# The seven-product last stage of a fused attention and two-MLP kernel: GpSimd's work moved to VectorE, other memory, other banks

## The chip, the cores and the metric

The kernel runs on one core of a Trainium2 chip. The metric is the device time of one execution in microseconds, the median of 3 runs. One more execution was taken by the profiler; its trace is what is read below. TensorE is called PE, VectorE DVE, ScalarE ACT, GpSimd POOL, SyncE SP.

## The reference, cut to what matters

Three blocks follow each other: attention with a memory term, an MLP, and a second MLP without an activation but with a product of two projections.

```python
x = attention(q, k, v, M_prev, z_prev, beta)          # (2304, 512)
h = x @ w_in                                          # 512 -> 2048
x2 = (h * np.tanh(np.log1p(np.exp(np.minimum(h, 20.0))))) @ w_out   # 2048 -> 512
a = x2 @ w1                                           # 512 -> 1024
b = x2 @ w2                                           # 512 -> 1024
out = ((a * b) @ w3) @ w_out2                         # 1024 -> 1024 -> 512
```

Inputs come as doubles and are decoded to float32 on the chip. Each float32 operand of a matmul is split into a rounded high part and a low part (high plus low is the value), and a product of two operands is made of three matmuls: high with high, high with low, low with high.

## The kernel before

The first MLP runs in four quarters of its 2048 columns (`emit_h`, `emit_x2`, the gate). Beside the last quarter a generator, `fold`, makes `w3 @ w_out2` (1024 x 512) in 32 pieces: decode (`decode`, L87 to L107: six DVE instructions and one POOL add per piece, three buffers for the loads), transpose, split, eight accumulated steps, then `wo` (L600 to L606), which has one buffer, is copied by ACT and DVE and stored to `w_dram`. When all is stored, `wft` is loaded from `w_dram` in two halves of two 1 MB loads (L657), into the memory that held `w_out2`, so the first half starts when the fold's last matmul is done.

The last stage then works on `x2` (512 x 2304, feature by token) in three column groups `c` of 768 tokens and eight row blocks `m` of 128 rows of `w1` and `w2`, 24 steps `k = 8c + m` in all. The products `a` and `b` of a step are not computed by eight block products but by seven, in Strassen's manner with common sums (`emit_ab`): seven operands made of the four quarters of a column group's `x2` (`quad`, `sums`, `operand`), seven blocks of weights made earlier and kept in `wc_dram` (`combine`), and sums of the seven results.

- `load_wc(k)` (L610) loads the seven weight blocks of row block `m` (896 KB) into one of three slots, three steps ahead; `split_wc(k)` (L616) splits them: ACT rounds (L619), POOL subtracts (L620), in two pieces of 1024 and 768 columns. It is done for all 24 steps, so three times for each block.
- `sums` and `operand` (L675 to L691): POOL makes differences of quarters, ACT rounds an operand (L686), DVE subtracts (L65). The first two operands live in `first` (pool `late`, which takes the memory of the fold's pool), the other five in `room`, the memory of the gate's last quarter of weights (L700).
- A product (L759) is six matmuls with 384 columns into one of the two F banks. After product `j` its result is read: `e1`, `e5` are copied by ACT, the others are added by DVE (L771), one add is POOL's. In step `m = 7` the next column group's operand `j` is made right after the reading of product `j`.
- At the end of a step DVE multiplies the two sums (L795), ACT rounds (L798) and DVE subtracts, into a ring of three slots.
- `emit_out(k, i)` (L731) multiplies slot `k` with `wft`: three matmuls of 512 columns for each of six token blocks, accumulated over the eight steps of a column group in three A and three X banks. It stands two steps behind the products, one block after each product from the second on. After `m = 7` ACT copies the bank (`ob`) and SP stores it.

`queued` fixes the order of these matmuls on PE. All other order is set by a planner: it simulates the engines, and each engine takes, in order of the program text, what the simulation says is ready, ahead of earlier text that is not. Each engine then executes its list in order. Tiles that share memory wait for all uses of the earlier tile.

## Time and profile before

| what | value |
|---|---|
| median of 3 runs | 1098.9 us (1098.56 to 1099.48) |
| the profiled execution's own time | 1100.98 us |
| its span, first to last instruction | 1098.8 us |
| mean granted PE clock | 0.981 |
| PE busy | 1022.8 us (93%) |
| DVE busy | 789.6 us (72%) |
| ACT busy | 578.9 us (53%) |
| POOL busy | 496.4 us (45%) |

The busy shares are means over stages with different limits; the last stage, from about 782 us to the end, is read by itself. In the answers "us" counts from the span's start; a row `[4.23 <-DVE ca L771]` says that the engine was idle for 4.23 us before the instruction and what released it. A row with x6 stands for six merged instructions.

### The profile page before, as it was taken

Reading aid. Unit: us, or ns where it says so; the run is one execution under the profiler, and the core shown is the slowest. Engines: PE = TensorE matmul, PEld = TensorE weight load, DVE = VectorE, ACT = ScalarE, POOL = GpSimd, SP = SyncE. Lnnn points to the kernel's source line nnn. Section 1 sums busy time; section 2 is a strip of 40 time slices with the busy share of each in tenths; the row PEclk is TensorE's granted clock in tenths of the full one; section 3 lists DMA queues with packets and bytes.
Section 4 is the critical chain, followed back from the end, with each engine's and each line's share of the span. In section 5 each row is a group of like instructions: output and inputs, shape, how many; then the busy total and the mean of one; then the engine's idle time right before and its main releaser. Section 6 shows DMA issues by size and latency. Waiting matters only on the chain. (4 is left out here: it accounts for less than half of the span.)

```text
span 1098.8 us, 17700 instructions
## 1 busy us (share of the span) xinstructions
PE 1022.8 (93%) x6368; PEld 873.8 (80%) x6368; DVE 789.6 (72%) x1677; ACT 578.9 (53%) x1169; POOL 496.4 (45%) x445
## 2 busy tenths in 40 slices
PE   7999999999999999999999998997499889989997
PEld 4565565557899899999999898895389779978996
DVE  5999998655798578976677788787455765575552
ACT  5777786776676556565566564642132433333312
POOL 6677657431465434444335232222345644454440
PEclk9999999999999999999999999999699999989999
DMA  6434434211333433334321732322421213212201
GB/s 147 113 93 106 115 91 119 61 25 42 108 95 117 147 96 105 106 92 130 112 77 49 254 108 83 108 68 76 172 101 68 98 66 108 89 68 97 95 34 58
DMA packets 115591, 107.06 MB, mean 97 GB/s; under 512 B 70192, under 2 KB 90672, under 8 KB 115504
## 3 DMA queue, kind: packets, MB, share of 16 engines
q1 hardware_dynamic: 115504, 105.94, 31.4%
q8 instruction: 50, 0.82, 0.3%
q14 instruction: 37, 0.30, 0.1%
HBM read 85.46 MB, written 20.45 MB: 96 GB/s over the span
## 5 line engine op out<-in xcount | busy, mean ns | idle before, releaser
L106 POOL TENSOR_TENSOR da<-da,de 128x512 f32<-128x512 f32 (+1 forms) x88 | 102.1, 1164 | 285.3 <-DVE de L105 262.5
L59 PE MATMUL psX<-gh,wqt 128*128 128x288 f32 x1024 | 209.8, 298 | 13.1 <-DVE x L558 7.8
L59 PEld LDWEIGHTS psX<-gh,wqt 128*128 128x128 f32 x1024 | 165.6, 189 | 17.4 <-DVE x L558 9.2
L620 POOL TENSOR_TENSOR wct<-wct 128x1024 fp32r<-128x1024 f32 (+1 forms) x48 | 106.4, 2237 | 123.8 <-ACT wct L619 123.8
L59 PE MATMUL psF<-room,wct 128*128 128x384 f32 x720 | 147.8, 341 | 10.2 <-ACT e L782 6.6
L59 PE MATMUL psX<-gl,wqt 128*128 128x288 f32 x512 | 151.2, 296 | 0.0
L59 PEld LDWEIGHTS psF<-room,wct 128*128 128x128 f32 x720 | 130.3, 189 | 23.4 <-ACT e L782 9.4
L59 PE MATMUL psA<-xt,wqt 128*128 128x288 f32 x840 | 121.7, 296 | 1.7 <-DVE y L467 1.7
L59 PEld LDWEIGHTS psA<-xt,wqt 128*128 128x128 f32 x840 | 115.0, 188 | 4.5 <-DVE y L467 2.8
L361 ACT ACTIVATE s<-s,acc 128x384 f32<-128x384 f32 (+3 forms) x144 | 84.9, 593 | 35.5 <-DVE acc L356 21.3
L99 DVE TENSOR_SCALAR da<-draw 128x512 int32<-128x512 int32 (+1 forms) x88 | 48.7, 557 | 70.8 <-DMA wc_dram<-da 18.7
L59 PEld LDWEIGHTS psX<-gl,wqt 128*128 128x128 f32 x512 | 96.8, 189 | 0.5
L776 ACT COPY e<-psF 128x384 f32<-128x384 f32 x24 | 11.5, 478 | 140.3 <-PE psF L59 112.2
L59 PE MATMUL psF<-first,wct 128*128 128x384 f32 x288 | 60.7, 361 | 23.9 <-ACT first L686 13.5
L356 DVE CUSTOM_DVE_ANT_0 s<-psA,mask 128x512 f32<-128x512 f32 (+2 forms) x144 | 65.0, 478 | 21.3 <-PE psA L59 19.1
L470 ACT CAST gh<-y 128x576 fp32r<-128x576 f32 x64 | 43.1, 675 | 66.8 <-DVE y L467 53.1
L59 PE MATMUL psF<-xt,wqt 128*128 128x288 f32 x552 | 77.5, 295 | 0.8 <-DVE y L467 0.8
L59 PEld LDWEIGHTS psF<-first,wct 128*128 128x128 f32 x288 | 55.0, 203 | 28.9 <-ACT first L686 13.9
L59 PEld LDWEIGHTS psF<-xt,wqt 128*128 128x128 f32 x552 | 74.5, 188 | 1.2 <-DVE y L467 1.0
L59 PE MATMUL psX<-pt,raw 128*64 128x64 f32 (+4 forms) x576 | 75.0, 328 | 0.0
L59 PE MATMUL psA<-kt,qt 64*128 64x384 f32 (+3 forms) x256 | 71.1, 485 | 2.5 <-DVE acc L356 2.0
L411 ACT COPY pt<-psF 128x512 f32<-128x512 f32 (+1 forms) x112 | 58.9, 543 | 26.3 <-PE psF L409 22.5
(124 smaller groups left out, 2178.8 us busy)
## 6 DMA issues: line engine op xcount, KB each, us to landing
wct<-wc_dram SPq DMA_DIRECT2D x24, 896.0 KB, 4.6
draw<-in_moe_w_out_dram SPq DMA_DIRECT2D x24, 512.0 KB, 3.6
draw<-in_moe_w_in_dram SPq DMA_DIRECT2D x16, 512.0 KB, 4.0
draw<-in_moe_w_dram SPq DMA_DIRECT2D x16, 512.0 KB, 3.9
draw<-in_moe_w_dram SPq DMA_DIRECT2D x32, 256.0 KB, 2.9
out_dram<-ob SPq DMA_DIRECT2D x18, 256.0 KB, 2.0
raw<-in_q_dram SPq DMA_DIRECT2D x32, 128.0 KB, 2.8
raw<-in_k_dram SPq DMA_DIRECT2D x32, 128.0 KB, 3.2
```

What stands on the lines that cost most here:

```text
L59: return nc.tensor.matmul(o, lhsT=l, rhs=r, start=start, stop=stop)
L99: V.tensor_scalar(out=ai, in0=hw, scalar1=0x7FFFFFFF, scalar2=None, op0=ALU.bitwise_and)
L106: nc.gpsimd.tensor_tensor(out=a, in0=a, in1=e, op=ALU.add)
L356: nc.vector.tensor_tensor_reduce(out=s, in0=o, in1=m, op0=ALU.add, op1=ALU.min, scale=-scale, scalar=init, accum_out=a,)
L361: nc.scalar.activation(out=s, in_=s, func=AF.Exp, scale=-1.0, bias=a, accum_out=r)
L411: nc.scalar.copy(out=t[:, 0:n], in_=o[:, 0:n])
L470: nc.scalar.copy(out=gh, in_=y[i])
L620: nc.gpsimd.tensor_tensor(out=w[:, 1, j], in0=f(w[:, 1, j]), in1=f(w[:, 0, j]), op=ALU.subtract)
L776: nc.scalar.copy(out=e1, in_=o)
```

## The change

- `split_wc` is called for the first eight steps only; DVE subtracts in place of POOL. The split block, both parts (1792 KB), is stored to a new buffer `ws_dram`, and later steps load it from there in two loads, without a split.
- `sums`, `operand` and the add to `cb` are done by DVE. For the first column group the operands are made in the order 5, 0, 1, 2, 3, 4, 6 and one difference is made in place.
- `first` and the temporaries are allocated in the pool that takes the memory of the gate's buffers (`wp3`), after the last gate product instead of ahead of it; one buffer `tmp` of four parts holds all sums of a step, several of them in the same part one after another.
- Products go to the A banks; the outputs' accumulators are three X, two F and one A bank.
- The ring has four slots (three and one more in `late`) and the outputs stand three steps behind.
- `sums` of the next column group are made at `m = 4` instead of `m = 5`.

```diff
--- before.py
+++ after.py
@@ -137,6 +137,7 @@
 
     NM = FF2 // 128
     wc_dram = dram.tile([NM, 128, 7, 2, 128], F32, name="wc_dram")
+    ws_dram = dram.tile([NM, 128, 2, 7, 2, 128], F32, name="ws_dram")
 
     def predecode():
         def light(c):
@@ -611,13 +612,19 @@
         w = wc[k] = xp.tile(
             [128, 2, 7, 2, 128], F32R, tag=f"xs{k % SLOTS}", name="wct", padded_shape=[128, 2, 9, 2, 128]
         )
-        dm(out=f(w[:, 1]), in_=wc_dram[k % NM])
+        if k < NM:
+            dm(out=f(w[:, 1]), in_=wc_dram[k])
+        else:
+            for i in range(2):
+                dm(out=f(w[:, i]), in_=ws_dram[k - NM if k < 2 * NM else k - 2 * NM, :, i])
 
     def split_wc(k):
         w = wc[k]
         for j in (slice(0, 4), slice(4, 7)):
             nc.scalar.copy(out=w[:, 0, j], in_=f(w[:, 1, j]))
-            nc.gpsimd.tensor_tensor(out=w[:, 1, j], in0=f(w[:, 1, j]), in1=f(w[:, 0, j]), op=ALU.subtract)
+            sub(w[:, 1, j], f(w[:, 1, j]), w[:, 0, j])
+        for i in range(2):
+            dm(out=ws_dram[k, :, i], in_=f(w[:, i]))
 
     folding = fold()
     pre0 = iter(())
@@ -650,7 +657,6 @@
     fk.close()
     T = 384
     late = ctx.enter_context(tc.tile_pool(name="late", bufs=1))
-    first = late.tile([128, 2, 2, 2, T], F32R, name="first")
     wft = wq.tile([128, 2, NM, DM], F32R, tag="wq0", name="wft")
     for s in range(2):
         for i in range(2):
@@ -663,55 +669,63 @@
 
 
 
+    emit_x2(prev, pre0)
+    wk.close()
+
+    wp3 = ctx.enter_context(tc.tile_pool(name="wp3", bufs=1, side="right"))
+    RING = 4
+    LAG = RING - 1
+    ring3 = xp.tile([128, 3, 2, 2 * T], F32R, tag="xs3", name="ring")
+    ring1 = late.tile([128, 2, 2 * T], F32R, name="ring1")
+    t2s = late.tile([128, 2, T], F32, name="t2")
+
+    def ring(k):
+        return ring3[:, k % RING] if k % RING < 3 else ring1
+
     K1, K2 = slice(0, 2), slice(2, 4)
-    t2 = late.tile([128, 2, T], F32, name="t2")
-    xo = [first[:, 0], first[:, 1]]
+    first = wp3.tile([128, 2, 2, 2, T], F32R, name="first")
+    room = w2q[0].tile([128, 2, KD + KQ, FQ], F32R, tag="wq1", name="room").rearrange("p i k f -> p (i k f)")
+    xo = [first[:, 0], first[:, 1]] + [
+        room[:, 4 * T * j:4 * T * j + 4 * T].rearrange("p (i k t) -> p i k t", i=2, k=2) for j in range(5)
+    ]
 
     def quad(c):
         t0 = 2 * T * c
-        return [x2[:, k, t0 + T * h:t0 + T * h + T] for k in (K1, K2) for h in range(2)]
-
-    def pool_sub(o, x, y):
-        nc.gpsimd.tensor_tensor(out=o, in0=x, in1=y, op=ALU.subtract)
+        b = [x2[:, k, t0 + T * h:t0 + T * h + T] for k in (K1, K2) for h in range(2)]
+        return b + [t2s if c else b[3]]
+
+    def minus(o, x, y):
+        nc.vector.tensor_tensor(out=o, in0=x, in1=y, op=ALU.subtract)
 
     def sums(c):
-        b11, b12, b21, b22 = quad(c)
-        pool_sub(b12, b12, b11)
-        pool_sub(t2, b22, b12)
+        b11, b12, b21, b22, t2 = quad(c)
+        minus(b12, b12, b11)
+        if c:
+            minus(t2, b22, b12)
 
     def operand(c, j):
 
-        b11, b12, b21, b22 = quad(c)
+        b11, b12, b21, b22, t2 = quad(c)
         src = (b11, t2, b21, b12, b11, b22, b21)[j]
         nc.scalar.copy(out=xo[j][:, 0], in_=src)
         sub(xo[j][:, 1], src, xo[j][:, 0])
         if j == 0:
-            pool_sub(b11, t2, b11)
+            minus(b11, t2, b11)
         if j == 2:
-            pool_sub(b21, b21, t2)
-
+            minus(b21, b21, t2)
+        if c == 0 and j == 5:
+            minus(t2, b22, b12)
+
+    split_wc(0)
     sums(0)
-    for j in range(2):
+    for j in (5, 0, 1, 2, 3, 4, 6):
         operand(0, j)
-    emit_x2(prev, pre0)
-    wk.close()
-
-    wp3 = ctx.enter_context(tc.tile_pool(name="wp3", bufs=1, side="right"))
-    room = w2q[0].tile([128, 2, KD + KQ, FQ], F32R, tag="wq1", name="room").rearrange("p i k f -> p (i k f)")
-    xo += [
-        room[:, 4 * T * j:4 * T * j + 4 * T].rearrange("p (i k t) -> p i k t", i=2, k=2) for j in range(5)
-    ]
-    for j in range(2, 7):
-        operand(0, j)
-    RING = 3
-    ring = xp.tile([128, RING, 2, 2 * T], F32R, tag="xs3", name="ring")
+        if j == 3:
+            split_wc(1)
 
     NC = NT // (2 * T)
     work = [(c, m) for c in range(NC) for m in range(NM)]
     outs = {}
-
-    def tmp(tag, n=1):
-        return wp3.tile([128, n, T], F32, tag=tag, name=tag, bufs=1)
 
     before = []
 
@@ -731,9 +745,9 @@
     def emit_out(k, i):
 
         c, m = work[k]
-        t = ring[:, k % RING]
+        t = ring(k)
         if m == 0 and i == 0:
-            outs[c] = [bank(tag) for tag in "AAAXXX"]
+            outs[c] = [bank(tag) for tag in "XXXFFA"]
         o = outs[c][i]
         ts = slice(128 * i, 128 * i + 128)
         queued(
@@ -742,22 +756,22 @@
             (o, t[:, 1, ts], wft[:, 0, m], False, m == NM - 1),
         )
         if m == NM - 1:
-            ob = wp3.tile([128, DM], F32, tag="ob", name="ob", bufs=2)
+            ob = late.tile([128, DM], F32, tag="ob", name="ob", bufs=2)
             nc.scalar.copy(out=ob, in_=o)
             t0 = 2 * T * c + 128 * i
             dm(out=out[t0:t0 + 128, :], in_=ob)
 
-    LAG = RING - 1
-
     def emit_ab(k):
         c, m = work[k]
         w = wc.pop(k)
-        e1, e5 = tmp("e1")[:, 0], tmp("e5")[:, 0]
-        u2, u3 = tmp("u2")[:, 0], tmp("u3")[:, 0]
-        ca, cb = tmp("ca", 2), tmp("cb", 2)
+        tmp = wp3.tile([128, 4, T], F32, tag="tmp", name="tmp", bufs=1)
+        ca, cb = tmp[:, 0:2], tmp[:, 2:4]
+        u2 = ca[:, 1]
+        e1 = u3 = cb[:, 0]
+        e5 = cb[:, 1]
 
         def product(j):
-            o = psF()[:, 0:T]
+            o = psA()[:, 0:T]
             x = xo[j]
             for kk in range(2):
                 queued(
@@ -767,8 +781,8 @@
                 )
             return o
 
-        def plus(o, x, y, eng=nc.vector):
-            eng.tensor_tensor(out=o, in0=x, in1=y, op=ALU.add)
+        def plus(o, x, y):
+            nc.vector.tensor_tensor(out=o, in0=x, in1=y, op=ALU.add)
 
         for j in range(7):
             o = product(j)
@@ -783,30 +797,28 @@
             elif j == 4:
                 plus(u3, o, u2)
                 plus(u2, u2, e5)
-                plus(cb[:, 1], u3, e5, nc.gpsimd)
+                plus(e5, u3, e5)
             elif j == 5:
-                plus(ca[:, 1], o, u2)
+                plus(u2, o, u2)
             else:
-                plus(cb[:, 0], o, u3)
+                plus(u3, o, u3)
             if m == NM - 1 and c + 1 < NC:
                 operand(c + 1, j)
             if j and k >= LAG:
                 emit_out(k - LAG, j - 1)
         nc.vector.tensor_tensor(out=ca, in0=ca, in1=cb, op=ALU.mult)
-        t = ring[:, k % RING]
+        t = ring(k)
         pr = ca.rearrange("p h t -> p (h t)")
         nc.scalar.copy(out=t[:, 0], in_=pr)
         sub(t[:, 1], pr, t[:, 0])
 
-    for k in range(2):
-        split_wc(k)
     for k, (c, m) in enumerate(work):
         emit_ab(k)
         if k + SLOTS < len(work):
             load_wc(k + SLOTS)
-        if k + 2 < len(work):
+        if k + 2 < NM:
             split_wc(k + 2)
-        if m == NM - 3 and c + 1 < NC:
+        if m == NM - 4 and c + 1 < NC:
             sums(c + 1)
     for k in range(len(work) - LAG, len(work)):
         for i in range(6):
```

## Rows read from the trace of the kernel before

**Rows 1.** busy us by stretch: length, PE, PEld, DVE, ACT, POOL, clock, DMA, GB/s
```profile
680.00:720.00 40.00, 38.66 (x259) 36.24 (x258) 32.67 (x77) 22.42 (x41) 12.39 (x11) 1.00 0.32 103
747.00:769.00 22.00, 15.77 (x60) 10.94 (x60) 16.11 (x42) 5.22 (x12) 4.24 (x5) 0.92 0.18 60
769.00:782.00 13.00, 0.00 (x0) 0.00 (x0) 0.85 (x2) 1.14 (x3) 0.32 (x1) 0.59 0.57 202
807.00:863.00 56.00, 56.00 (x291) 51.99 (x290) 30.94 (x40) 16.89 (x24) 27.46 (x16) 1.00 0.22 81
863.00:898.00 35.00, 26.41 (x126) 23.19 (x125) 28.64 (x25) 11.99 (x17) 19.96 (x9) 0.95 0.15 53
```
**Rows 2.** timeline of PE in step 6: start us, length us, instructions
```profile
854.37 1.22 PE L59 MATMUL psF<-room,wct 128*128 128x384 f32 x6
855.44 0.86 PE L59 MATMUL psA<-wft,ring 128*128 128x512 f32 x3
856.13 1.22 PE L59 MATMUL psF<-room,wct 128*128 128x384 f32 x6
```
**Rows 3.** timeline of PE at the starts of steps 7-9 and 15-17
```profile
863.17 2.26 PE L59 MATMUL psF<-first,wct 128*128 128x384 f32 x12
...
880.43 2.23 PE L59 MATMUL psF<-first,wct 128*128 128x384 f32 x6 [4.23 <-DVE ca L771]
...
897.38 2.26 PE L59 MATMUL psF<-first,wct 128*128 128x384 f32 x12
...
966.98 2.26 PE L59 MATMUL psF<-first,wct 128*128 128x384 f32 x12
...
984.23 4.21 PE L59 MATMUL psF<-first,wct 128*128 128x384 f32 x12 [4.23 <-DVE ca L771]
...
1002.74 1.57 PE L59 MATMUL psF<-first,wct 128*128 128x384 f32 x8
```
**Rows 4.** groups of DVE, 807 to 863 us: busy us, mean ns, idle before
```profile
L771 DVE TENSOR_TENSOR u<-u,e 128x384 f32<-128x384 f32 x5 | 8.1, 1621 | 0.5
...
L65 DVE TENSOR_TENSOR ring<-ca,ring 128x768 fp32r<-128x768 f32 x5 | 4.8, 951 | 0.4 <-ACT ring L798 0.4
...
L771 DVE TENSOR_TENSOR u<-psF,u 128x384 f32<-128x384 f32 x5 | 2.8, 557 | 14.1 <-PE psF L59 14.1
```
**Rows 5.** the same in 863 to 898 us
```profile
L65 DVE TENSOR_TENSOR room<-x,room 128x768 fp32r<-128x768 f32 x5 | 12.1, 2411 | 0.0
```
**Rows 6.** timeline of the fold's end: SP, ACT, PE's first product
```profile
768.84 0.91 SPq L657 DMA_DIRECT2D wft<-w_dram  x2
769.85 9.69 SPq L603 DMA_DIRECT2D w_dram<-wo  x2
778.32 0.37 ACT L601 CAST wo<-psF 128x256 fp32r<-128x256 f32 x1 [9.11 <-DMA w_dram<-wo]
...
782.33 0.69 PE L59 MATMUL psF<-first,wct 128*128 128x384 f32 x1 [13.53 <-ACT first L686]
```
**Rows 7.** the chain that ended last, its last piece on PE
```profile
1090.25 2.05 PE psX L59 x9
```
**Rows 8.** timeline of POOL, a split of weight block 2
```profile
697.64 4.55 POOL L620 TENSOR_TENSOR wct<-wct 128x1024 fp32r<-128x1024 f32 x2 [5.33 <-ACT wct L619]
```
**Rows 9.** groups by form in 747 to 782 us, DVE
```profile
L65 DVE TENSOR_TENSOR room<-x,room 128x768 fp32r<-128x768 f32 x3 | 3.2, 1128 | 0.0
```
**Rows 10.** DMA queue, 354.9 to 362.4 us: packets, MB, share of 16 engines
```profile
q1 hardware_dynamic: 2270, 1.91, 81.8%
```
**Rows 11.** DMA issues: 807 to 863 us, then 740 to 1099 us
```profile
wct<-wc_dram SPq DMA_DIRECT2D x5, 896.0 KB, 4.5
...
w_dram<-wo SPq DMA_DIRECT2D x6, 256.0 KB, 2.1
```
**Rows 12.** timeline of DVE and PE where step 5 begins
```profile
842.82 0.95 DVE L65 TENSOR_TENSOR ring<-ca,ring 128x768 fp32r<-128x768 f32 x1
...
844.53 1.22 PE L59 MATMUL psF<-room,wct 128*128 128x384 f32 x6
```

## The prediction

> **What bounds the kernel now.** I read the table of stages first [rows 1]. In the last stage the middle stretch, 807 to 863 us, has TensorE busy for all of its 56 us at the full granted clock (1.00, the 2.4 GHz level), while VectorE is busy for 31. There nothing but TensorE's own work counts. Its rhythm [rows 2]: a product starts at 854.37, an output block at 855.44, the next product at 856.13. So a product (6 matmuls) takes 1.07 us, an output block (3 matmuls) 0.69, 0.23 a matmul. Seven products are 7.5 us and six blocks 4.1, together one step: the six steps between 897.38 and 966.98 give 69.6/6 = 11.6 us [rows 3]. No edit of the change removes a matmul, so these 11.6 stay.
>
> What can be won is where TensorE waits. The table shows three such places.
>
> First, the two changes of column group. Step 7 starts at 863.17 and step 9 at 897.38; that is 34.2 us for two steps that should take 23.2. Step 15 starts at 966.98 and step 17 at 1002.74: 35.8. The excess is 11.0 + 12.6 = 23.6 us, and the longest waits in it, 4.2 us at 880.43 and at 984.23, end on a VectorE add [rows 3]. The groups of VectorE say why. A subtract of 768 columns takes 951 ns where it stands alone and 2411 ns in the transition, where GpSimd is working; the add of two buffers takes 1621 ns, while an add that reads a PSUM bank takes 557 even there [rows 4, 5]. VectorE is busy for 28.6 of 35 us [rows 1] mostly because its instructions with two buffers are stretched while GpSimd works.
>
> Second, the start. The fold's last matmul is followed by 13.5 us without one: ScalarE casts `first` only when the last `wo` store has landed, because `first` takes the fold's memory. That store stood behind two 1 MB loads of `wft`, and the second `wo` cast waited 9.1 us for it [rows 6].
>
> Third, the steps just behind that. Step 7 starts at 863.17, while 782.33 and seven steps of 11.6, less the outputs that the first two don't have (8.2), would give 855.3. So 7.9 us of waits lie in the first steps.
>
> After the last matmul (1092.30) come 6.5 us of copies and stores to 1098.8 [rows 7].
>
> **The change, part by part.**
>
> *Start.* `first` and the temporaries move into the gate's memory, which is free when the last gate product is done, at about 747. The planner moves work forward as soon as its inputs are there: the split of weight block 2, written behind step 0, ran at 697.64 [rows 8]. So I expect the operands of the first column group, and the products of step 0, to fill the fold's tail from 747 on, where TensorE is busy for 15.8 of 22 us and then idle for 13 [rows 1]. What is late next is VectorE. Its list from 747 to the end of step 2:
> the fold's rest, 16.1 + 0.85 us less the 3.2 us of `room` subtracts in it = 13.8 [rows 1, 9];
> seven operand subtracts and three differences at 0.95 = 9.5 (the fourth, `b12`, can go earlier);
> three steps at five PSUM adds of 0.557, two buffer adds of 0.56 (the second is the one taken from GpSimd; 384 columns, by the PSUM add, the nearest row), a multiply and a ring subtract of 0.95 each = 5.8, so 17.4;
> the splits of blocks 3 and 4. A split is a subtract of 768 columns, 0.951, and one of 1024; from (951 − 557)/384 = 1.03 ns a column I estimate 1.21 for that, so 2.2 each and 4.3 for both.
> Sum 45.0, so 792. I add 3 us for gaps in the chains and 3 for half of the `wo` wait: the store still goes behind the `wft` loads, ScalarE and VectorE take instructions in order, and whatever is queued behind the second `wo` cast waits up to 6.5 us. Between both ends I take half. Step 3 then starts at 798. Bounds: TensorE alone would need 747 + 15.8 + 3 × 7.5 = 785; the `wo` wait in full and 8 us a step from 782.33 give 806.
>
> *Weights.* Blocks 0 to 2 are split earlier, on VectorE instead of GpSimd: 3 × 2.2 us in a stretch where VectorE is busy for 32.7 of 40 us and TensorE for 38.7 [rows 1]. I cost it at nothing, since GpSimd's two subtracts there (4.55 us [rows 8]) stretched VectorE too; if nothing hides it, 6.6 us. In steps 1 to 5 the split adds 2.2 to VectorE's 5.8 of 11.6. The slot of a block becomes free only when its store has landed too. A store and a load in one step are 1.84 + 0.92 = 2.76 MB; a stretch with seven stores into the weight buffer moved 1.91 MB in 81.8% of 7.5 us, 311 GB/s, hence 8.9 us of 11.6 [rows 10]. The load alone lands in 4.5 us [rows 11]. Slots are reloaded three steps ahead, so I cost it at nothing. Bounds: none, or the price of the small stores (rival 4). From step 8 on both halves are read, 5.9 us of a step, and ScalarE's and VectorE's splits are gone. The Trainium skill, page "DMA: Bandwidth & Descriptors", section Specifications, gives a limit of some 358 GB/s for one core at HBM; by that a store is an estimated 5.1 us against 5.9 by the row, and the sum is the same.
>
> *Transitions.* Step 7 adds seven subtracts and two differences at 0.95 = 8.6 to VectorE's 5.8, 14.4 in a step of 11.6; the excess of 2.8 runs into step 8, whose operands have 10 us of slack. A product's bank must be read before the second next product starts, which leaves 0.69 + 1.07 + 0.69 − 0.56 = 1.9 us. The backlog in between stays near 1 us. I take 1.5 us lost per transition, 3.0 instead of 23.6; bounds 0 and 8 for both (2.8 plus a late chain, each).
>
> *Banks, one temporary.* Products now go through the A banks, of which the outputs hold one: two, as many as before. All sums share one buffer, so the first add of a step, into `ca`, must wait for the ring subtract of the step before. That subtract starts at 842.82 and the fourth product (the bank's next user is the product at 844.53) starts 1.7 us later; subtract and add need 0.95 + 0.56 = 1.5 [rows 12]. That leaves 0.2. I take 2 us for all steps; bounds 0 and 1 us on each of 21 steps.
>
> *Outputs three steps behind.* Six blocks move from step 2 to the end: 54 matmuls at 0.23 = 12.4 us after the last product. Nothing is added in all.
>
> **Sum.** 798 + 21 × 11.6 (steps 3 to 23) + 12.4 + 3.0 + 2 + 6.5 = 1065.5, a span of about 1065 against 1098.8. The profiled execution itself took 1100.98, 2.2 more than its span, while the median of the runs is 1098.9, so span and median agree and I predict a median of 1065 us.
>
> **The rivals.** (1) *The start doesn't move:* the second `wo` cast stands ahead of the operands in ScalarE's and VectorE's queues, so that step 3 starts at 806 or later. For it speaks that ScalarE stood behind that cast for 9.1 us [rows 6]; against it the three `room` subtracts that ran in the middle of the fold [rows 9]. 1073 to 1076.
> (2) *The shared temporary decides:* 0.5 to 1 us per step, 1065 + 10 to 21 = 1075 to 1086. For it the slack of 0.2 us; against it that the subtract can go ahead of the add that stood before it, since both are ready early.
> (3) *The clock stays low at the start.* TensorE was granted 0.92 in the fold's tail and 0.59 in the gap [rows 1], and twelve product matmuls at half rate took 4.21 us, 0.35 each [rows 3]. At 1.2 GHz three steps are 3 × 42 × 0.35 = 44 us, so 747 + 15.8 + 44 = 807 for step 3, 1074 in all. Products paced by VectorE leave such gaps; against it, products fill the pauses of the fold. The Trainium skill, page "TensorE: Matmul & The Clock Gate", section "What's actually happening", calls the throttled state the default that activity releases; the granted clock in the rows agrees.
> (4) *Slower: the stores of the split weights hold slots and queue.* No row shows a store of this size. If it went at the rate of the `wo` stores, 256 KB in 2.1 us [rows 11], a store would take 14.7 us. The three early ones would hold up the fold's decode loads; if its three buffers keep these 8 us ahead (an assumption), by 6.7 each, 20 us on TensorE's path; then five stores, five loads at 4.5 and 14 us of `wft` (4.2 MB at 311 GB/s) make 110 us, so step 8 at 879 instead of 856, 23 more: 1108. Linear in the store's time, it reaches the time of before at about 13.5 us a store. Against it the 311 GB/s [rows 10].
>
> **Chances.** Forecast 0.70, with its own range 1052 to 1076; rival 1 0.10, rival 2 0.07, rival 3 0.03, rival 4 0.10, of which 0.02 near its turning point. Runs of this kernel differ by under 1 us, so that 0.2% (2.2 us) is about what can be told from no change. Faster 0.90, within 0.2% 0.02, slower 0.08. The range that holds 8 in 10 takes in rivals 1 and 3 and half of rival 2: 1050 to 1084.
>
> **What would show it.** Right: the first product starts between 752 and 769; the buffer subtracts take 0.95 us throughout; step 7 to step 9 in under 26 us; 11.6 us steps in between; the stores of split weights land in about 6 us. Wrong: product matmuls only from 779 on (1); a wait of the products on the ring subtract's successor at each step (2); granted clock near 0.5 in the first steps (3); casts waiting for weight loads, or decode waiting for its loads (4).

## The result and the profile after

| | before | after |
|---|---|---|
| median | 1099.2 us (4 runs, 1098.56 to 1101.69) | 1079.7 us (4 runs, 1079.02 to 1080.81) |
| ratio | 1 | 0.9819, 95% interval 0.9802 to 0.9837 |
| span | 1098.8 us | 1078.2 us |
| PE, DVE, POOL busy | 1022.8, 789.6, 496.4 us | 1022.2, 764.6, 335.6 us |

The forecast was 1065 us, in a range of 1050 to 1084 (1052 to 1076 for its own sum, the rest for rivals). The gain of 19.5 us is there, but it is 14.7 us smaller than forecast: the time lies in the wide range and outside the narrow one. That it came no further off is in part luck, because errors of both signs stood in the sum.

By stretches (columns as in [rows 1]; the fourth is steps 3 to 5, the fifth steps 7 and 8):

```profile
680.00:720.00 40.00, 40.00 (x271) 37.71 (x270) 31.67 (x85) 23.15 (x43) 6.66 (x9) 1.00 0.48 154
747.00:769.00 22.00, 18.10 (x87) 16.28 (x88) 19.47 (x45) 6.91 (x12) 2.59 (x4) 0.92 0.41 152
769.00:782.00 13.00, 12.28 (x60) 11.22 (x58) 8.41 (x15) 4.39 (x8) 1.02 (x2) 0.87 0.32 114
785.70:829.12 43.42, 37.78 (x182) 33.39 (x182) 25.07 (x37) 11.00 (x16) 0.00 (x0) 0.96 0.83 314
841.53:869.56 28.03, 24.25 (x121) 21.26 (x120) 19.90 (x29) 9.14 (x13) 0.00 (x0) 1.00 0.35 132
```

The gap of 13 us in the fold's tail is filled: TensorE is busy for 12.28 of 13.00 us where [rows 1] has 0.00. Steps 7 and 8 take 28.0 us instead of 34.2. And two things that no step of the forecast had: TensorE is busy for all of 40 us in 680 to 720 (38.66 before), and the DMA engines are busy for 0.83 of steps 3 to 5.

PE where steps begin, in answer to [rows 3], with the waits of step 3:

```profile
785.70 2.24 PE L59 MATMUL psA<-first,wct 128*128 128x384 f32 x12
788.29 0.50 PE L59 MATMUL psX<-wft,ring 128*128 128x512 f32 x1 [0.35 <-DMA wft<-w_dram]
791.00 0.73 PE L59 MATMUL psX<-wft,ring 128*128 128x512 f32 x2 [2.21 <-DMA wft<-w_dram]
...
802.40 2.00 PE L59 MATMUL psA<-first,wct 128*128 128x384 f32 x7 [1.87 <-DVE tmp L785]
...
841.53 1.74 PE L59 MATMUL psA<-first,wct 128*128 128x384 f32 x9
...
855.92 1.31 PE L59 MATMUL psA<-first,wct 128*128 128x384 f32 x6 [0.79 <-DVE tmp L785]
...
869.56 2.26 PE L59 MATMUL psA<-first,wct 128*128 128x384 f32 x12
...
881.98 1.22 PE L59 MATMUL psA<-first,wct 128*128 128x384 f32 x6
...
894.91 1.40 PE L59 MATMUL psA<-first,wct 128*128 128x384 f32 x7
...
906.51 1.74 PE L59 MATMUL psA<-first,wct 128*128 128x384 f32 x9
...
1059.16 2.23 PE L59 MATMUL psX<-wft,ring 128*128 128x512 f32 x9
```

Step 3 starts at 785.70, 12.3 us ahead of the forecast. Step 9 takes 12.42 us (869.56 to 881.98) and not 11.6; step 11 (894.91 to 906.51) does take 11.60. Behind 1059.16 come 19.0 us, as forecast (18.9).

The start of step 9 on all engines shows the 0.82 us:

```profile
869.56 2.26 PE L59 MATMUL psA<-first,wct 128*128 128x384 f32 x12
869.65 0.96 DVE L809 TENSOR_TENSOR tmp<-tmp 128x768 f32<-128x768 f32 x1
870.65 0.83 ACT L812 CAST ring<-tmp 128x768 fp32r<-128x768 f32 x1 [6.38 <-DVE tmp L809]
871.51 0.96 DVE L65 TENSOR_TENSOR ring<-tmp,ring 128x768 fp32r<-128x768 f32 x1 [0.90 <-ACT ring L812]
871.66 0.86 PE L59 MATMUL psX<-wft,ring 128*128 128x512 f32 x3
872.56 0.48 ACT L790 COPY tmp<-psA 128x384 f32<-128x384 f32 x1 [1.08 <-DVE ring L65]
873.07 0.56 DVE L785 TENSOR_TENSOR tmp<-psA,tmp 128x384 f32<-128x384 f32 x1 [0.60 <-ACT tmp L790]
873.09 1.31 PE L59 MATMUL psA<-room,wct 128*128 128x384 f32 x6 [0.57 <-ACT tmp L790]
```

To be read from the bottom: the third product waits for a bank, that bank for ScalarE's copy of `e1` (L790), and the copy for the ring subtract (L65) of the step before. The copy writes `cb[:, 0]`; the subtract reads `ca`. They share no element, but `tmp` is allocated anew in each step, and the new buffer waits for all uses of the old. Steps 11 and 19 take 11.60 us all the same. There the outputs, three steps behind, change column group, so that their bank among the A banks is free for the products; that this third bank hides the copy's delay is argued, not tested.

VectorE in 842 to 870 us, in answer to [rows 4, 5] (busy us, mean ns, idle before):

```profile
L785 DVE TENSOR_TENSOR tmp<-psA,tmp 128x384 f32<-128x384 f32 x10 | 5.5, 554 | 5.6 <-PE psA L59 5.0 <-ACT tmp L790 0.6
L65 DVE TENSOR_TENSOR room<-x,room 128x768 fp32r<-128x768 f32 x5 | 4.8, 954 | 0.3 <-ACT room L710 0.2
...
L785 DVE TENSOR_TENSOR tmp<-tmp 128x384 f32<-128x384 f32 x4 | 2.2, 556 | 0.1
```

The operand subtract that took 2411 ns beside GpSimd takes 954; the add of two buffers takes 556, as the forecast took it. The stores, in 785.7 to 829 us, then the two halves of a block at 764 to 767 and of another at 798.3 to 801 us (KB each, median us to landing):

```profile
ws_dram<-wct SPq DMA_DIRECT2D x6, 896.0 KB, 4.6
wct<-wc_dram SPq DMA_DIRECT2D x3, 896.0 KB, 10.1
...
ws_dram<-wct SPq DMA_DIRECT2D x2, 896.0 KB, 3.6
...
ws_dram<-wct SPq DMA_DIRECT2D x2, 896.0 KB, 12.1
```

Half a split block lands in 3.6 us on a quiet queue and in 12.1 beside `wft` and the weight blocks. From the issue of the first half to the landing of the second it is 5.7 us for the block at 764 (the forecast's 5.9), but 12.8 and 16.0 us for those stored from 780.55 and 798.36. Rival 4 had 14.7 us for every store: its price came for two blocks, and its total of 1108 us did not.

Sorted by stage, span against span: step 7 begins 21.6 us earlier, the two changes of column group take 56.8 instead of 70.0 us, steps 9 to 14 take 4.6 us more, and what follows step 17's start 9.6 more (4.1 for six output blocks moved there, 5.5 for the waits of step 9's kind): −21.6 − 13.2 + 4.6 + 9.6 = −20.6.

### The profile page after: what moved, and what is told of

Its sections match the earlier page's. It is cut to its first block, busy times and chain, and to the rows that moved or that the text cites. A ratio compares the mean times of both kernels' runs of the same rounds, so it can differ in the third digit from the quotient of the medians.

```text
span 1078.2 us, 17570 instructions
## 1 busy us (share of the span) xinstructions
PE 1022.2 (95%) x6368; PEld 872.1 (81%) x6368; DVE 764.6 (71%) x1729; ACT 554.8 (51%) x1137; POOL 335.6 (31%) x361
## 5 line engine op out<-in xcount | busy, mean ns | idle before, releaser
L106 POOL TENSOR_TENSOR da<-da,de 128x512 f32<-128x512 f32 (+1 forms) x88 | 104.1, 1186 | 325.3 <-DVE de L105 287.8
L59 PE MATMUL psA<-room,wct 128*128 128x384 f32 x720 | 150.3, 346 | 19.4 <-ACT tmp L790 19.2
L59 PEld LDWEIGHTS psA<-room,wct 128*128 128x128 f32 x720 | 130.3, 192 | 36.9 <-ACT tmp L790 27.5
L785 DVE TENSOR_TENSOR tmp<-psA,tmp 128x384 f32<-128x384 f32 x120 | 66.1, 556 | 99.9 <-PE psA L59 87.5
L99 DVE TENSOR_SCALAR da<-draw 128x512 int32<-128x512 int32 (+1 forms) x88 | 45.5, 521 | 68.2 <-DMA wc_dram<-da 20.6
L812 ACT CAST ring<-tmp 128x768 fp32r<-128x768 f32 x24 | 20.0, 833 | 104.2 <-DVE tmp L809 98.0
L412 ACT COPY pt<-psF 128x512 f32<-128x512 f32 (+1 forms) x112 | 59.0, 544 | 26.5 <-PE psF L410 22.6
L410 PE MATMUL psF<-ident,s 128*128 128x128 f32 x400 | 64.9, 282 | 0.0
L59 PE MATMUL psX<-wft,ring 128*128 128x512 f32 x216 | 62.2, 401 | 2.6 <-DMA wft<-w_dram 2.6
```

The costliest lines, as they stand in the source:

```text
L59: return nc.tensor.matmul(o, lhsT=l, rhs=r, start=start, stop=stop)
L99: V.tensor_scalar(out=ai, in0=hw, scalar1=0x7FFFFFFF, scalar2=None, op0=ALU.bitwise_and)
L106: nc.gpsimd.tensor_tensor(out=a, in0=a, in1=e, op=ALU.add)
L410: nc.tensor.transpose(o[:, 128 * x:128 * x + 128], src[:, 128 * jb:128 * jb + 128], ident)
L412: nc.scalar.copy(out=t[:, 0:n], in_=o[:, 0:n])
L785: nc.vector.tensor_tensor(out=o, in0=x, in1=y, op=ALU.add)
```

## Experiments

Ratios are to the kernel before, run on the same chip at the same time. "The change" is the kernel after. The kernel before took 1099.2 us beside the change and 1099.7 to 1102.2 beside the experiments, so a difference between medians of two experiments is uncertain by some 2 us. The traces differ as well, and early: the fold's first matmul runs at 615.5 to 618.6 us, although TensorE, VectorE, ScalarE and GpSimd each work through the same list in every experiment on the change up to 627 us. Where a small difference of spans matters, it is therefore also counted from that matmul.

**1. One buffer for all steps.** Is it the new allocation, or the shared use of its parts?

```diff
+    tmp = wp3.tile([128, 4, T], F32, name="tmp")
...
     def emit_ab(k):
-        tmp = wp3.tile([128, 4, T], F32, tag="tmp", name="tmp", bufs=1)
```

> The changed kernel with the buffer of the sums allocated once, ahead of the steps, instead of anew in each step; nothing else. In the changed kernel's trace a step of the middle takes 12.42 us, not 11.6, and the copy of e1 waits for the ring subtract of the step before. Theory (release): a buffer that is allocated anew is free only when all uses of the last one are done, so e1 waits for the ring subtract although it overwrites another part; with one buffer it waits for the multiply alone. Then a middle step takes 11.6 us again, the wait of e1 on the ring subtract is gone, and the time is 1079.7 - 19 x 0.82 = about 1064 us. Rival (banks): two A banks are too few for the products whatever e1 waits for; then steps stay at 12.4 us and the time at 1079.

Measured: 1062.6 us (1061.82 to 1063.9), ratio 0.9644 [0.9630, 0.9659]; 17 us faster than the change by one line moved. PE:

```profile
789.10 0.80 PE L59 MATMUL psX<-wft,ring 128*128 128x512 f32 x1 [5.71 <-DMA wft<-w_dram]
791.82 1.22 PE L59 MATMUL psX<-wft,ring 128*128 128x512 f32 x2 [1.93 <-DMA wft<-w_dram]
802.85 2.26 PE L59 MATMUL psA<-first,wct 128*128 128x384 f32 x12
814.45 2.29 PE L59 MATMUL psA<-first,wct 128*128 128x384 f32 x12
```

Steps take 11.60 us, so the parts can be shared without loss and the allocation is the cause: shown. What is left over 11.6 us a step is 10.1 us in step 3 (781.15 to 802.85), which now waits 7.6 us for `wft`, and 6.2 us in the two transitions (3.3 and 2.8). Step 3 also starts 4.5 us earlier than in the change.

**2. The kernel before with such a buffer.** Does the same allocation cost as much with GpSimd's add in the chain?

```diff
-        e1, e5 = tmp("e1")[:, 0], tmp("e5")[:, 0]
-        u2, u3 = tmp("u2")[:, 0], tmp("u3")[:, 0]
-        ca, cb = tmp("ca", 2), tmp("cb", 2)
+        all4 = tmp("all", 4)
+        ca, cb = all4[:, 0:2], all4[:, 2:4]
+        u2 = ca[:, 1]
+        e1 = u3 = cb[:, 0]
+        e5 = cb[:, 1]
```

> The kernel before with that part alone: its six temporaries become one buffer of four parts, allocated anew in each step. Products still use the F banks, outputs stand two steps behind, GpSimd works as before. Theory (release): a middle step goes from 11.6 to about 12.4 us, the time from 1099 to about 1099 + 19 x 0.82 = 1115 us. Rival (banks): F banks are as many as before, so 11.6 us steps and 1099 us.

Measured: 1128.4 us, ratio 1.0244 [1.0225, 1.0263]. In the table of waits (us in all, times, longest), its PE has

```profile
PE psF L59 <- ACT all L778: 33.4, 23, 4.6
```

where the change has 19.2 us, 19 times, on the same copy. The direction held, the size was underrated by 13 us. A middle step takes 12.53 us (11.60 before), near the forecast, but steps 1 and 2 take 14.8 and 17.5 instead of 9.4 and 11.7: there the copy of `e1` comes behind the rounding of a weight block in ScalarE's list, and TensorE waits 4.55 and 3.98 us for it.

**3. No stored splits.** All 24 blocks are split by ScalarE and VectorE, nothing goes to `ws_dram`.

```diff
-        if k < NM:
-            dm(out=f(w[:, 1]), in_=wc_dram[k])
-        else:
-            for i in range(2):
-                dm(out=f(w[:, i]), in_=ws_dram[...])
+        dm(out=f(w[:, 1]), in_=wc_dram[k % NM])
...
-        for i in range(2):
-            dm(out=ws_dram[k, :, i], in_=f(w[:, i]))
...
-        if k + 2 < NM:
+        if k + 2 < len(work):
```

> The changed kernel without the buffer of split weights: every step loads the 896 KB block and splits it on ScalarE and VectorE, all 24 times; nothing is stored and loaded back. Theory (the stores crowd the queue in the first steps): the store of wo after the fold lands some 3 to 5 us earlier, step 3 shrinks from 16.7 us to 12 to 13, and VectorE still has room for 2.2 us more per step, so 1074 to 1079 us. Rival (splitting once is what makes room on VectorE): 16 more splits at 2.2 us stand in the way of the sums, 0.5 us or more per step, 1085 to 1095 us.

Measured: 1087.3 us, ratio 0.9873 [0.9852, 0.9894], 7.7 us slower than the change. PE:

```profile
788.96 2.24 PE L59 MATMUL psA<-first,wct 128*128 128x384 f32 x12
801.71 2.26 PE L59 MATMUL psA<-first,wct 128*128 128x384 f32 x12
...
839.09 2.26 PE L59 MATMUL psA<-first,wct 128*128 128x384 f32 x12
856.03 2.33 PE L59 MATMUL psA<-first,wct 128*128 128x384 f32 x12
872.86 2.26 PE L59 MATMUL psA<-first,wct 128*128 128x384 f32 x12
```

Step 3 takes 12.75 us instead of 16.7, but it starts 3.3 us later and ends only 0.7 earlier. Counted from the fold's first matmul it starts 1.5 us later and ends 2.4 earlier, so that not all of these 4 us are the price of the stores' bytes; step 7 starts 4.2 us earlier without the stores. But steps 7 and 8 take 33.8 us instead of 28.0, and steps 15 and 16 take 33.9 instead of 28.7: the splits go back on VectorE's list just where it is full. With the 70.0 us of before and 67.6 here, it is the absence of splits that shortens the transitions. Both theories were half right.

**4. GpSimd gets back its subtracts, differences and the add.**

```diff
-            sub(w[:, 1, j], f(w[:, 1, j]), w[:, 0, j])
+            sub(w[:, 1, j], f(w[:, 1, j]), w[:, 0, j], nc.gpsimd)
...
     def minus(o, x, y):
-        nc.vector.tensor_tensor(out=o, in0=x, in1=y, op=ALU.subtract)
+        nc.gpsimd.tensor_tensor(out=o, in0=x, in1=y, op=ALU.subtract)
...
-                plus(e5, u3, e5)
+                nc.gpsimd.tensor_tensor(out=e5, in0=u3, in1=e5, op=ALU.add)
```

> The changed kernel with GpSimd given back its part: the subtracts of the weight splits (eight blocks), the differences of operands and the add to the last sum. Memory, banks, stores and lag stay as changed. Theory (VectorE's two-buffer instructions are stretched while GpSimd works): the gate's last products end at 746 instead of 740, buffer subtracts beside GpSimd take 2.3 us instead of 0.95, each transition loses 4 us or more against now: 1090 to 1100 us. Rival (the start alone brought the gain): the time stays within 3 us of 1079.7.

Measured: 1092.3 us, ratio 0.9916 [0.9901, 0.9931]. The gate's last matmul is back at 747.4 us. Of the 13.6 us of span that are lost (11.4 from the fold's first matmul), 7.9 are there when step 3 starts (5.7), 2.1 more by step 7 and 3.0 in the first transition, from step 7 to step 9:

```profile
851.50 2.26 PE L59 MATMUL psA<-first,wct 128*128 128x384 f32 x12
...
882.57 2.26 PE L59 MATMUL psA<-first,wct 128*128 128x384 f32 x12
```

There VectorE has

```profile
L65 DVE TENSOR_TENSOR room<-x,room 128x768 fp32r<-128x768 f32 x5 | 6.8, 1364 | 1.3 <-ACT room L710 1.3
```

The second transition loses nothing (28.4 us instead of 28.7), where 4 us or more were expected in each. So in this layout GpSimd's work costs 2.7 us of the two transitions together; most of its price lies ahead of them.

**5. Only the split subtracts of blocks 0 to 2 back on GpSimd** (with one buffer). These run beside the gate's last products.

```diff
-            sub(w[:, 1, j], f(w[:, 1, j]), w[:, 0, j])
+            sub(w[:, 1, j], f(w[:, 1, j]), w[:, 0, j], nc.gpsimd if k < 3 else None)
```

> The kernel with one temporary allocated once, and the subtracts of the splits of weight blocks 0 to 2 given back to GpSimd. Theory (GpSimd's work beside the gate's last products stretches VectorE there): the gate's last products end at 745 to 748 us instead of 740, TensorE is busy for under 39 of 40 us in 680 to 720, and the time is 1066 to 1069. Rival (the earlier end of the gate comes from something else, or is swallowed by the wait for wft that follows): the gate ends at 740 to 742, or the time stays at 1062 to 1063.

Measured: 1065.5 us (1063.23 to 1066.52), ratio 0.9678 [0.9657, 0.9699]. All three signs moved the right way and each fell short: the gate's last matmul runs at 744.8 us (746.5 before, 740.3 in the change), and TensorE is busy for 39.64 of 40 us in 680 to 720, not under 39 (38.53 of 40 in 640 to 680; 40.00 in both with the splits on VectorE). The fold's first and the gate's last matmul, with one buffer alone, then in this kernel:

```profile
615.68 0.39 PE L59 MATMUL psF<-o,w3h 128*128 128x512 f32 x1
740.07 0.29 PE L59 MATMUL psX<-gl,wqt 128*128 128x288 f32 x1
...
617.59 0.39 PE L59 MATMUL psF<-o,w3h 128*128 128x512 f32 x1
744.82 0.29 PE L59 MATMUL psX<-gl,wqt 128*128 128x288 f32 x1
```

Of the 4.75 us at the gate's end 1.9 were there at the start; the splits cost 2.8 (124.4 us between the two matmuls, 127.2 here). The kernel before needs 129.6, and experiment 4, where the differences too are GpSimd's, 129.2. One group of the fold's decode on VectorE in 640 to 720 us, first in this kernel, then in the change:

```profile
L105 DVE SCALAR_TENSOR_TENSOR de<-draw,de 128x256 f32<-128x256 uint32 x15 | 9.9, 659 | 0.3
```

```profile
L105 DVE SCALAR_TENSOR_TENSOR de<-draw,de 128x256 f32<-128x256 uint32 x17 | 7.2, 422 | 0.3
```

The kernel before has 650 ns there. The mean hides how it comes about: 13 of the 15 take their 0.42 us, and the two that meet a split (4.4 and 4.3 us of GpSimd in 655 to 702) take 2.43 and 1.95. The second split:

```profile
697.10 4.34 POOL L65 TENSOR_TENSOR wct<-wct 128x1024 fp32r<-128x1024 f32 x2 [5.55 <-ACT wct L624]
697.62 2.13 DVE L104 TENSOR_SCALAR de<-da 128x256 int32<-128x256 int32 x1
699.78 1.95 DVE L105 SCALAR_TENSOR_TENSOR de<-draw,de 128x256 f32<-128x256 uint32 x1
```

So GpSimd's splits hold VectorE's decode, and that is 2.8 of the 5.2 us by which the change shortened this stretch; the differences, which experiment 4 gives back as well, are most of the rest. The delay goes through to the end: step 3 waits for `wft` as long as with one buffer alone (5.76 and 1.93 us), and the span counted from the fold's first matmul is 2.8 us longer (the medians differ by 3.0).

**6. `first` back in the fold's memory** (ring slot and `ob` change places with it).

```diff
-    ring1 = late.tile([128, 2, 2 * T], F32R, name="ring1")
+    ring1 = wp3.tile([128, 2, 2 * T], F32R, name="ring1")
...
-    first = wp3.tile([128, 2, 2, 2, T], F32R, name="first")
+    first = late.tile([128, 2, 2, 2, T], F32R, name="first")
...
-            ob = late.tile([128, DM], F32, tag="ob", name="ob", bufs=2)
+            ob = wp3.tile([128, DM], F32, tag="ob", name="ob", bufs=2)
```

> The changed kernel with `first` back in the memory of the fold's pool; one ring slot and the output copies take its place in the gate's memory. The sums' buffer is still allocated anew in each step. Theory (the start moved because first no longer waits for the stores of wo): the products of step 0 wait for the last wo store again and start at 780 or later instead of 743, step 3 starts at 800 or later instead of 785.7, and the time goes from 1079.7 to 1095 or more. Rival (the start is VectorE's list, which stays the same): within 4 us of 1079.7.

Measured: 1101.2 us, ratio 0.9996 [0.9984, 1.0008]; all of the change's gain is gone. The first product waits for the fold's last `wo` store again (782.33 before, 743.38 in the change):

```profile
777.93 0.69 PE L59 MATMUL psA<-first,wct 128*128 128x384 f32 x1 [12.98 <-ACT first L710]
```

**7. Products of step 1 held behind the fold's last matmul** (with one buffer): is it the fold, slowed by the products, that makes `wft` late?

```diff
+            if k == 1 and j == 0:
+                with tc.issue_after(folded[0].ins):
+                    o = product(j)
```

> The kernel with one buffer of sums (1062.6 us), and the products of step 1 placed behind the fold's last matmul in TensorE's order. There, step 3 starts at 781 but its first output block waits until 789 to 792 for wft, whose load starts when the fold's last matmul is done, at 781. Theory (products that run inside the fold delay the fold, and with it wft): the fold's last matmul is done at 770 to 774, wft is there when step 3 starts at 783 to 787, and the time is 1054 to 1059 us. Rival (VectorE's list sets the start, whatever the order): the fold ends earlier but steps 1 and 2 end later by as much, 1061 to 1064 us.

Measured: 1066.6 us, ratio 0.9680 [0.9659, 0.9702]. The wait for `wft` is gone, but the fold ends at 776.9 instead of 781 only, and step 3 starts at 794.6 instead of 781.2 and takes 13.9 us. So the products of step 1 delay the fold by some 5 us, but holding them loses more: in 745 to 777 us TensorE waits 7.5 us for the decode (GpSimd's add L106, behind VectorE), and the granted clock is 0.79 there.

**8. Outputs two steps behind** (with one buffer).

```diff
-    LAG = RING - 1
+    LAG = 2
```

> The kernel with one buffer of sums (1062.6 us), with the outputs two steps behind instead of three (the ring keeps four slots). Theory (the third step is cover for the load of wft): the output blocks come up at step 2, at about 770, wait there until 789 to 792 for wft, and step 2's other products, some 6 us, fall behind that wait: 1067 to 1070 us. Rival (the lag is worth nothing): 1061 to 1064 us.

Measured: 1066.6 us, ratio 0.9681 [0.9659, 0.9704]. The wait for `wft` moves to step 2 and grows from 7.6 to 12.1 us (9.04 and 3.02). The third step of lag is worth 4 us, by the landing of `wft`.

**9. The second difference of the next group held until the step ends** (with one buffer).

```diff
         if c:
-            minus(t2, b22, b12)
+            with tc.issue_after(ended[0].ins):
+                minus(t2, b22, b12)
```

> The kernel with one buffer of sums (1062.6 us), with the second difference of the next column group held until the end of step 4 (step 12) of the group before, instead of as early as the planner finds it ready. In the trace this difference, 0.96 us, stands in VectorE's list in the middle of the first transition (at 846 us), and at the start it waits there for the last wo store. Theory (VectorE's backlog sets the transition): the first transition, 14.0 + 12.5 us for two steps, becomes 1 us shorter, and the wait of VectorE at the start goes: 1060 to 1062 us. Rival: no difference, 1062.5.

Measured: 1062.8 us, ratio 0.9646 [0.9624, 0.9667], against 0.9644 without it: no difference. Steps 7 and 8 take 26.0 instead of 26.5 us.

**10. `wft` ahead in SP's order** (with one buffer). The store of split block 4 and the load of block 5 go behind the first two loads of `wft`.

```diff
+        if k == 5:
+            with tc.issue_after(half_in[1].ins):
+                dm(out=f(w[:, 1]), in_=wc_dram[k])
...
+        if k == 4:
+            with tc.issue_after(half_in[1].ins):
+                store_ws(k, w)
```

> The kernel with one temporary allocated once, and SP issues the first two loads of wft ahead of the store of the split block 4 and of the load of weight block 5. Theory (the outputs of step 0 wait in step 3 for wft, which stands behind some 2.7 MB of these transfers): wft lands about 787 to 788 us instead of 791.8, the waits of 5.7 and 1.9 us at 789 to 792 mostly go, step 3 takes 15 us or less instead of 21.7, and the time is 1056 to 1060. Rival (the wait is taken over by the second wo cast and what VectorE and ScalarE have queued behind it, or by weight block 5, which now lands later): step 3 or 4 keeps the loss and the time stays at 1062 to 1063.

Measured: 1061.6 us, ratio 0.9641 [0.9618, 0.9663]: the rival. PE waits 5.8 instead of 7.6 us for `wft`, and ScalarE stands for weight block 5:

```profile
792.46 1.79 ACT L629 CAST wct<-wct 128x1024 fp32r<-128x1024 f32 x2 [7.79 <-DMA wct<-wc_dram]
```

**11. `wft` in pieces** (with one buffer). The first outputs read an eighth of `wft`; those two loads of 256 KB go first.

```diff
+    load_wft(0, 1)
+    with tc.issue_after(stored[-2].ins):
+        load_wft(1, 4)
+    load_wft(4, 8)
```

> The kernel with one temporary allocated once, and the rows of wft that the outputs of step 0 read (two loads of 256 KB) go first; behind them SP issues weight block 5, the store of the fold's last half but one, the other rows of wft's first half, and the store of the split block 4. Theory (step 3 loses its time to the landing of 2 MB of wft, of which its first outputs need a quarter, and in the kernel with the reordered queue to ScalarE's queue behind the late weight block): no wait for wft over 2 us, the second wo cast by 788 us, step 3 in 14 us or less instead of 21.7, time 1053 to 1056. Rival (whatever lands last of these 4 MB is what ScalarE, which works in order, stands behind): step 3 and 4 still take 31 us or more together and the time stays at 1060 to 1063.

Measured: 1063.8 us, ratio 0.9672 [0.9655, 0.9688]: the rival again. Step 3 takes 15.7 us, but step 4 takes 18.95, behind the fold's last store:

```profile
805.93 0.96 DVE L717 TENSOR_TENSOR t<-x 128x768 f32<-128x768 f32 x1 [6.68 <-DMA w_dram<-wo]
```

That store (256 KB) took 10.3 us behind four of 896 KB.

**12. The same with the fold's last two stores first,** then weight block 5, the rest of `wft`, and last the split blocks 4 and 5; ScalarE casts the last `wo` ahead of block 5.

```diff
-    with tc.issue_after(stored[-2].ins):
+    with tc.issue_after(stored[-1].ins):
         load_wft(1, 4)
...
-            with tc.issue_after(half_in[1].ins):
+            with tc.issue_after(stored[-2].ins):
                 dm(out=f(w[:, 1]), in_=wc_dram[k])
...
-        if k == 4:
+        if k in (4, 5):
```

> As the kernel with wft in pieces, but the last two stores of the fold go ahead of weight block 5, of the other rows of wft and of the stores of the split blocks 4 and 5, and ScalarE makes the second wo cast ahead of the split of block 5. Theory (in the kernel with wft in pieces step 4 took 18.95 us because the fold's last store landed only at some 806, behind 3.6 MB of split weights, and DVE's t and ScalarE's ring, which take the fold's memory, waited 6 us for it): that store lands by 794, no instruction of ScalarE or VectorE waits over 2 us for it, steps 3 and 4 take 28 us or less together (34.6 there, 33.3 in the kernel with one temporary alone), and the time is 1054 to 1058. Rival (in this stretch the DMA engines are full at some 410 GB/s, and whatever is put last makes the wait): another wait of 5 us or more, for the weight blocks or the rest of wft, takes its place by step 8, and the time stays at 1060 to 1064.

Measured: 1056.5 us (1055.04 to 1059.21), ratio 0.9591 [0.9569, 0.9612]: the fastest kernel here, and its interval lies clear of that of one buffer alone. Steps 3 and 4 take 25.8 us together (33.3 there). In the table of stretches, first one buffer alone, then this kernel:

```profile
790.00:800.00 10.00, 8.18 (x33) 7.52 (x34) 3.00 (x5) 0.85 (x2) 0.00 (x0) 0.72 0.81 296
```

```profile
790.00:800.00 10.00, 9.15 (x48) 8.21 (x47) 6.74 (x10) 2.41 (x4) 0.00 (x0) 1.00 0.97 320
```

In the same 10 us TensorE executes 48 matmuls instead of 33. Two waits of the theory's kind stayed over its 2 us (2.78 us of VectorE for the store, 3.37 of ScalarE for block 5), and 2.1 us came back in step 6; ScalarE's longest wait there (5.2 us, before the ring cast) ends right behind VectorE's multiply and holds no one. By the ratios the gain over one buffer is 5.8 us. The profiled spans (1057.4 against 1060.0) differ by 2.6 only, but the fold's first matmul runs at 618.6 us here and at 615.7 there, with the same order of instructions on these four engines up to 785 us; counted from it the gain is 5.5 us.

## Why the prediction was right or wrong

| term | forecast | after | one buffer |
|---|---|---|---|
| step 3 starts | 798 | 785.7 | 781.2 |
| 21 steps of 11.6 | 243.6 | 243.6 | 243.6 |
| over that, steps 3 to 6 | 0 | 9.4 | 10.1 |
| both transitions | 3.0 | 10.4 | 6.2 |
| shared temporary, other steps | 2 | 10.1 | 0 |
| after the last product | 18.9 | 19.0 | 18.9 |
| sum | 1065.5 | 1078.2 | 1060.0 |

**The direction and the largest step held.** Moving `first` out of the fold's memory is worth some 20 us (experiment 6: 19.5 by the ratios, 21.7 by the spans), as much as the whole net gain. The operands and step 0's products did fill the fold's tail, from 743.4 us on and so ahead of the 752 to 769 that were forecast. Of the other signs of being right the subtracts of 0.95 us came; the two steps of a transition in under 26 us and the steps of 11.6 us came only with one buffer, and the first of these not quite (26.5 and 26.0).

**The start was 12.3 us too late,** for two reasons. "*Weights.* I cost it at nothing" let the gate end at about 747. It ended at 740: 5.2 of these 6 us are GpSimd's work taken away from beside the gate, 2.8 the splits alone (experiment 5). The row with the reason was at hand: [rows 1] showed TensorE at 38.66 of 40 us beside 12.39 us of GpSimd, and I had read it as nothing to gain. The second is the 6 us added for gaps and half of the `wo` wait: that wait came, but only after step 3 had started. The list of 45.0 us counted from 741 gives 786, near the 785.7 measured, but that is luck. VectorE was busy for only 37.2 of the 45.1 us from 740.6 on, the multiply and the ring subtract of step 2 came after step 3 had started, and with one buffer step 3 starts at 781.2: 4.5 us of this start are the price of the allocation too.

**The shared temporary failed in mechanism and size.** "The first add of a step, into `ca`, must wait for the ring subtract" named the elements that are shared. The program waits for more, the whole buffer, so that the first to be held is ScalarE's copy of `e1`, which comes before that add. It costs 0.82 us a step: 10.1 us outside the transitions, some 4 inside (10.4 against 6.2) and 4.5 before step 3, where 2 was taken in all. Rival 2 had the price (0.5 to 1 us a step, 1075 to 1086) and the time fell into its bounds, but by another wait than the one it named. That tiles in one memory wait for all uses of the earlier one was known of this kernel; I applied it to `first` and not to `tmp`.

**The landing of `wft` had no term.** I had it only as a share in rival 4. With the products 20 us earlier, the first outputs come before `wft` has landed. The change waits 2.6 us for it, since its step 3 starts later; with one buffer it is 7.6 us. Experiments 10 to 12 show that it is a matter of order: these 20 us of a nearly full queue can be arranged so that no one stands behind them for long, but moving one transfer only hands the wait to the next.

**The transitions** kept to their bounds (0 to 8) without the allocation: 6.2 against 3.0. But the reason that the forecast gave for their length failed. VectorE's instructions were stretched beside GpSimd (2411 ns), yet taking GpSimd away alone does not shorten the two transitions: with a split in every step on VectorE and none of this work on GpSimd they take 67.6 us (experiment 3; 70.0 before), with GpSimd's work given back but no splits in later steps 59.5 (experiment 4; 56.8 in the change). All but the 70.0 hold some 4 us of the allocation. The transitions shrank because the splits of later steps are gone. One difference held back changed nothing (experiment 9); which of VectorE's instructions delays the products there is open.

**Stores and lag.** Rival 4's price of 14.7 us for a store was right for two blocks in the crowded stretch (12.8 and 16.0) and off by a factor of 2.6 on a quiet queue (5.7); its place was right. The stores cost 4.2 us up to step 7 and pay 10.9 at the transitions (experiment 3). The third step of lag pays as cover for `wft` (experiment 8), not as forecast for nothing. Not tried by themselves are the banks and the order of the first operands.

## What to carry to other kernels

Allocate a temporary that lives through a loop once, ahead of it: a new allocation of the same memory waits for the last use of every part of the old one, also where the parts written first are long free. When a change moves work ahead, list the transfers that it now meets, in queue order and with their bytes, and put first the one that most instructions stand behind. Work that is needed in several steps with the same result, here the splits, is worth storing where its engine's list is full, even if the stores cost time elsewhere. An engine that only feeds idle resources can still slow the one that paces the end: look at what is stretched beside it before costing its removal at nothing.

## What the runs showed of the hardware

- A mix of loads and stores moved 412 GB/s over 790 to 800 us in experiment 11 and 416 in experiment 10, with the 16 DMA engines full. The forecast had taken 311 from [rows 10]. The Trainium skill, page "DMA: Bandwidth & Descriptors", section Specifications, gives about 358 GB/s as one core's limit at HBM; the measurement is above it.

```profile
790.00:800.00 10.00, 7.55 (x40) 6.81 (x39) 5.98 (x9) 2.91 (x5) 0.00 (x0) 1.00 1.03 412
```

- Here a wait cost TensorE more than its length: with one buffer the clock granted in 790 to 800 us was 0.72, a mean of its two levels (1.2 and 2.4 GHz), after 7.6 us of waits. Step 3 lost 10.1 us, 2.5 more than these; the product at 792.84 us took 1.92 us up to the next output block instead of 1.07.
- Beside GpSimd's subtracts a VectorE instruction with two buffers as inputs (L105) went from 0.42 to 1.95 and 2.43 us, while an add that reads a PSUM bank stayed at 554 to 557 ns. The Trainium skill, page "SBUF — State Buffer", section "Who interferes with whom", says that an instruction with two SBUF inputs contends with GpSimd's reads; the trace agrees. It shows that some instructions with one input are held as well: L104 took 2.13 us instead of 0.29 (experiment 5). That this reached TensorE 20 us and more before the stage that was changed is what I had not expected.
